# Chunked attention by pairs of tiles, with its 64x64 products on all four quarters of the array

## The chip, the cores and the metric

One core of one Trainium2 chip runs one program. The metric is the device time of that core in microseconds (us), as the median of several runs. TensorE is called PE below (PEld is its weight load), VectorE DVE, ScalarE ACT, GpSimd POOL, and SP is the engine that issues most of the DMAs.

## The reference

Three stages follow each other; only the first is touched by the change. Attention is taken within chunks of 64 positions, apart for each of 8 batches and 8 heads:

```python
q_c = q.reshape(B, H, nc, 64, D)            # B, H, S, D = 8, 8, 576, 64, float32; k_c, v_c alike
scores = scale * np.matmul(q_c, k_c.transpose(0, 1, 2, 4, 3))
attn = np.exp(scores - np.max(scores, axis=-1, keepdims=True))
attn = attn / (np.sum(attn, axis=-1, keepdims=True) + 1e-09)
out = np.matmul(attn, v_c)                  # then heads side by side: x of [8, 576, 512]
```

The second stage, called the mixing here, shifts `x` by one position, blends it with two vectors, and multiplies by `w_k` (512x1024), `w_v` (1024x512) and `w_r` (512x512): `sigmoid(xr @ w_r) * (relu(xk @ w_k)**2 @ w_v)`. The third stage gates 4 experts, each a causal attention over all 576 positions with a head of 64.

## The kernel before

A **tile** is 128 positions, so two chunks `c` of 64, with all 8 heads, which are kept as 4 pairs `g` of two heads `e`. There are 36 tiles. For a tile the kernel runs four steps:

- `s_T` transposes q and k on PE (4 + 4 products with the identity) into PSUM and copies them to SBUF on ACT. Each transposed tile has head `e` of a pair on partitions 64e to 64e+63. k is copied in two halves into a buffer `KB` that holds zeros outside two diagonal blocks, so that one product with 128 rows gives the scores of both heads of a pair.
- `s_S` makes the scores: 8 products (4 pairs of heads, 2 chunks) of 128 rows, 64 columns of weights and 128 columns that stream; chunk `c` lands on partitions 64c to 64c+63. DVE then takes the maximum (L158), subtracts it (L160), ACT takes the exponential (L161), DVE sums (L163), adds 1e-9 (L164), inverts (L165), and DVE or POOL multiplies (L166).
- `s_PT` transposes the result (4 products) and ACT copies it.
- `s_PV` multiplies with v: 16 products of 64 rows, 64 columns of weights and 64 streamed columns. In each, rows and output partitions belong to the same head `e`, so only the two quarters of the array on its diagonal are used. ACT copies the result into the unit's `XT`.

All of these are float32. The trace shows two records on PE for each float32 product that is not a transpose, and one for a transpose: 16 for the scores of a tile, 32 for its products with v.

A **unit** is 384 positions, three tiles; there are 12. The mixing of a unit is 240 products of 128 rows, 128 columns of weights and 384 streamed columns, in lines L57 to L59 (tile `mps`); 2,880 in all. Its weights come from HBM as 64-bit floats and are made into two 32-bit parts by 40 **conversions** of 128x256, four DVE instructions each (L290, L291, L292, L294), besides work on ACT and POOL. Conversions, attention and the mixing of unit 0 are interleaved at the start of the program. After that a credit per mixing item (`rate0`, `rate`; 20 items a unit) lets attention steps in, up to `xb` = 4 units ahead. The list `attn` holds the steps with a lag of two tiles: T of tile t, PT of t-2, S of t, PV of t-2. A scheduler that works with a timeline of its own moves instructions within this; on the chip each engine runs its instructions in the order that it wrote.

PSUM has eight banks: three for the mixing, and five for attention, given as 3 for transposes, 1 for scores, 1 for products with v.

Of the kernel before, what the change touches and what calls it, by code (L numbers as in the profile page):

```python
# [8 lines left out]
F32 = mybir.dt.float32  # L9
F32R = mybir.dt.float32r  # L10
# [10 lines left out]
CH = 64  # L21
UNIT = 384
CFG = dict(ps=(2, 3, 1, 2), P=5, sm=3, load=6, lag=(3, 4), out=(5, 1), qk1=(1, 1), qk0=(10, 1.2), v=(11, 1), order=(3, 4, 0, 1, 2), after=1, conv='v', clo='g', x2hi='g', x2lo='v', ylo='g', yhi='v', xt='aa', r2='av', klo='vg', slo='gv', d='gg', amul='vg', nearly=2, x2b=1, yb=4, qb=4, direct=((0, 1), (1, 1), (1, 1)), tailAV=4, kp=1, yt=1, yf=2, zb=1, om=(4, 3, 2, 1, 0), hp=1000, x2d=2, early=3, rate0=0.65, rate=0.7, sh=(10, 12, 2), sh2=(11, 1, -1), pro=(24, 0.4, 20, 18), alag=2, seq=0, end=2, outL=(10, 2), outE=2, first='qqcvcvcv', kcp='aa', dsc='v', ldb=2, vb=3, cn=256, stb=3, xb=4, pa=(3, 1, 1), cb=2)
# [38 lines left out]
def attn_mix(tc, at, x2T, q, k, v, mu_k, mu_r, w_k, w_v, w_r, ident, attended_all, mixed_k):  # L62
# [14 lines left out]
    with ExitStack() as ctx:  # L77
# [28 lines left out]
        def load_v(t):  # L106
            x = at.tile([128, 2, HP, D], F32, tag="ldv", bufs=CFG["vb"], name="ldv")
            for c in range(2):
                b, s = divmod(t * 128 + c * CH, S)
                for e in range(2):  # L110
                    nc.sync.dma_start(out=x[e * 64:(e + 1) * 64, c],
                                      in_=v[b, e::2, s:s + CH, :].rearrange("g p d -> p g d"))
            qkv["v", t] = x

        qT, kT, PP, PT, XT = {}, {}, {}, {}, {}

        KB = [at.tile([128, HP, 2, 128], F32, tag=f"kT{i}", bufs=1, name="kT") for i in range(2)]
        for x in KB:
            for e in range(2):
                r = slice(e * 64, e * 64 + 64)  # L120
                nc.gpsimd.memset(x[r, :, :, 64 - e * 64:128 - e * 64], 0.0)
        seen = []
        nT = NU * TPU

        def s_T(t):
            with tc.issue_after(seen[-1].ins) if seen and t < CFG["seq"] else nullcontext():
                s_T2(t)

        def s_T2(t):
            for nm, dst in (("q", qT), ("k", kT)):  # L130
                src = qkv.pop((nm, t))
                p = pa.tile([128, HP, 128], F32, tag="T", bufs=CFG["pa"][0], name="Tps")
                for g in range(HP):
                    nc.tensor.transpose(p[:, g], src[:, g * 128:(g + 1) * 128], ident)  # L134
                if nm == "q":
                    o = at.tile([128, HP, 128], F32, tag="qT", name="qT")
                    nc.scalar.activation(out=o, in_=p, func=ACTF.Copy)
                else:
                    o = KB[t % 2]
                    for e in range(2):  # L140
                        r = slice(e * 64, e * 64 + 64)
                        copy(nc, CFG["kcp"][e], o[r, :, :, r], p[r].rearrange("p g (c k) -> p g c k", c=2))
                dst[t] = o
            if t + CFG["ldb"] < nT:
                load_qk(t + CFG["ldb"])

        def s_S(t):
            a, b = qT.pop(t), kT.pop(t)
            p = pa.tile([128, H * CH], F32, tag="S", bufs=CFG["pa"][1], name="Sps")
            for g in range(HP):  # L150
# [4 lines left out]
            p = p.rearrange("p (h k) -> p h k", h=H)  # L155
            seen.append(last)
            m = at.tile([128, H], F32, tag="m", name="m")
            nc.vector.tensor_reduce(m, p, axis=AXX, op=ALU.max)  # L158
            e = at.tile([128, H, CH], F32, tag="P", name="P")
            nc.vector.tensor_tensor(e, p, m.unsqueeze(2).to_broadcast([128, H, CH]), op=ALU.subtract)  # L160
            nc.scalar.activation(out=e, in_=e, func=ACTF.Exp, scale=scale)  # L161
            z = at.tile([128, H], F32, tag="z", name="z")
            nc.vector.tensor_reduce(z, e, axis=AXX, op=ALU.add)  # L163
            nc.vector.tensor_scalar(z, z, 1e-9, None, op0=ALU.add)  # L164
            nc.vector.reciprocal(z, z)  # L165
            eng(nc, CFG["amul"][t // TPU >= CFG["nearly"]]).tensor_tensor(e, e, z.unsqueeze(2).to_broadcast([128, H, CH]), op=ALU.mult)  # L166
            PP[t] = e

        def s_PT(t):
            e = PP.pop(t).rearrange("p h k -> p (h k)")  # L170
            p = pa.tile([128, HP, 128], F32, tag="T", bufs=CFG["pa"][0], name="PTps")
            for g in range(HP):
                nc.tensor.transpose(p[:, g], e[:, g * 128:(g + 1) * 128], ident)
            o = at.tile([128, HP, 128], F32, tag="PT", name="PT")
            nc.scalar.activation(out=o, in_=p, func=ACTF.Copy)
            PT[t] = o

        def s_PV(t):
            a = PT.pop(t)
            vt = qkv.pop(("v", t))  # L180
            p = pa.tile([128, HP, 128], F32, tag="PV", bufs=CFG["pa"][2], name="PVps")
            for g in range(HP):
                for c in range(2):
                    for e in range(2):
                        r = slice(e * 64, e * 64 + 64)
                        cc = slice(c * CH, (c + 1) * CH)
                        nc.tensor.matmul(out=p[r, g, cc], lhsT=vt[r, c, g], rhs=a[r, g, cc],  # L187
                                         start=True, stop=True)
            u, i = divmod(t, TPU)
            if i == 0:  # L190
                XT[u] = wkr.tile([128, HP, NSEG, SEG + 1], F32, tag="XT", bufs=CFG["xb"], name="XT")
            x = XT[u]
            g0, done = i * 2, 0
            while done < 2:
                sg, o = divmod(g0 + done, CPS)
                n = min(2 - done, CPS - o)
                copy(nc, CFG["xt"][u >= CFG["nearly"]], x[:, :, sg, 1 + o * CH:1 + (o + n) * CH], p[:, :, done * CH:(done + n) * CH])
                done += n
            if t + CFG["vb"] < nT:
                load_v(t + CFG["vb"])  # L200
# [119 lines left out]
        lag = CFG["alag"]  # L320
        for t in range(nT + lag):
            if t < nT:
                attn.append((t // TPU, s_T, t))
            if t >= lag:
                attn.append(((t - lag) // TPU, s_PT, t - lag))
            if t < nT:
                attn.append((t // TPU, s_S, t))
            if t >= lag:
# [550 lines left out]
```

## Time and profile before

| | us |
|---|---|
| median of 3 runs (1089.34 to 1090.14) | 1089.36 |
| the profiled execution, its own time | 1086.98 |
| span of its trace | 1085.2 |
| TensorE busy | 1040.5 |
| VectorE busy | 747.2 |
| ScalarE busy | 612.9 |
| GpSimd busy | 451.4 |

The span is the time from the first to the last instruction in the trace. Busy time is the union of an engine's instructions; TensorE's instructions are pipelined, so the start of one to the start of the next says what one costs, and not its own duration.

### The profile page before, as it was taken

How to read it: one execution, taken by the hardware profiler on the slowest of the kernel's cores; microseconds unless marked ns; L12 is line 12 of the kernel's file. 1: busy time of each engine (PE TensorE's matmuls, PEld its weight loads, DVE VectorE, ACT ScalarE, POOL GpSimd, SP SyncE). 2: the span in 40 equal slices, each digit the busy share in tenths (PEclk: the TensorE clock that was granted, in tenths of full speed). 3: DMA queues.
4: the chain of work that ended last, by engine and by line, in shares of the span. 5: the costliest groups of instructions: out<-in, count | busy, mean ns of one | idle time of the engine just before them, and what ended most of it. 6: DMA issues, size and time to landing. Idle time of an engine off the chain costs nothing.

```text
span 1085.2 us, 21428 instructions
## 1 busy us (share of the span) xinstructions
PE 1040.5 (96%) x7846; PEld 979.8 (90%) x7846; DVE 747.2 (69%) x1910; ACT 612.9 (56%) x1457; POOL 451.4 (42%) x569
## 2 busy tenths in 40 slices
PE   5788899999999999999999999999999999999997
PEld 4676689999999999999999999999999898999985
DVE  5999994465554746463646652488697787878996
ACT  5778767242244646363535324266776667666774
POOL 2574663355553535353535453632331232423101
PEclk8999999999999999999999999999999999999999
DMA  9847673101103232414121311852742535254312
GB/s 194 202 105 177 178 187 89 59 1 59 53 17 93 55 98 50 111 41 112 40 69 24 85 44 35 178 149 54 182 119 85 150 66 178 56 160 114 89 52 70
DMA packets 170401, 105.23 MB, mean 97 GB/s; under 512 B 133832, under 2 KB 146232, under 8 KB 170296
## 3 DMA queue, kind: packets, MB, share of 16 engines
q1 hardware_dynamic: 134904, 54.56, 20.2%
q0 software_dynamic: 35392, 49.30, 17.3%
q8 instruction: 63, 1.03, 0.4%
q14 instruction: 42, 0.34, 0.1%
HBM read 66.01 MB, written 28.38 MB: 87 GB/s over the span
## 4 chain that ended last, share of the span: by engine, by line
PE 70%; DVE 16%; DMA 5%; ACT 3%; issue 3%; SPq 2%; POOL 1%; ACTq 0%; DVEq 0%; POOLq 0%
PE mps L57 14%; PE mps L59 14%; PE mps L58 14%; PE pj L57 4%; PE pj L58 4%; PE pj L59 4%; PE Tps L654 3%; PE PVps L187 2%; PE AVps L678 2%; PE Sps L153 2%; DMA out_dram<-o 2%; PE AVps L674 2%; PE Tps L134 2%; DVE sm L596 1%; PE Sps L594 1%
## 5 line engine op out<-in xcount | busy, mean ns | idle before, releaser
L218 POOL TENSOR_TENSOR xa<-XT 128x384 f32<-128x384 f32 x96 | 92.7, 974 | 106.2 <-DVE xlr L229 75.6
L57 PE MATMUL mps<-xhk,wkh 128*128 128x384 f32 x384 | 132.1, 345 | 1.8 <-ACT wkh L306 1.8
L57 PE MATMUL mps<-kh,wvh 128*128 128x384 f32 x384 | 130.1, 345 | 1.4 <-ACT wvh L306 1.4
L58 PE MATMUL mps<-xlk,wkh 128*128 128x384 f32 x384 | 129.6, 337 | 0.0
L59 PE MATMUL mps<-xhk,wkl 128*128 128x384 f32 x384 | 128.9, 340 | 0.0
L59 PE MATMUL mps<-kh,wvl 128*128 128x384 f32 x384 | 127.5, 338 | 0.7 <-POOL wvl L307 0.7
L58 PE MATMUL mps<-kl,wvh 128*128 128x384 f32 x384 | 127.7, 336 | 0.0
L256 DVE TENSOR_TENSOR r<-r 128x384 f32<-128x384 f32 x80 | 68.0, 850 | 68.2 <-ACT r L249 68.0
L258 POOL TENSOR_TENSOR kl<-r,kh 128x384 fp32r<-128x384 f32 x80 | 86.7, 1086 | 65.4 <-ACT kh L257 60.9
L606 ACT ACTIVATE P<-sm,nm 128x128 f32<-128x128 f32 (+4 forms) x160 | 91.3, 571 | 37.9 <-DVE nm L596 22.2
L227 DVE SCALAR_TENSOR_TENSOR xa<-xa,mu,XT 128x384 f32<-128x384 f32 x96 | 88.8, 939 | 19.5 <-POOL xa L218 19.4
L596 DVE CUSTOM_DVE_ANT_0 sm<-Sps,mask 128x192 f32<-128x192 f32 (+3 forms) x192 | 83.5, 438 | 14.0 <-PE Sps L594 12.2
L257 ACT ACTIVATE kh<-r 128x384 fp32r<-128x384 f32 x96 | 50.5, 526 | 63.8 <-DVE r L256 63.4
L654 PE MATMUL Tps<-ident,P 128*128 128x128 f32 x480 | 81.3, 275 | 1.7 <-DVE PT00l L658 0.8
L515 POOL DMA_DIRECT2D K<-Kp x64 | 34.2, 547 | 110.7 <-ACT Kp L508 110.1
L57 PEld LDWEIGHTS mps<-xhk,wkh 128*128 128x128 f32 x384 | 72.1, 188 | 4.2 <-ACT wkh L306 2.5
L57 PEld LDWEIGHTS mps<-kh,wvh 128*128 128x128 f32 x384 | 71.9, 188 | 4.2 <-ACT wvh L306 2.0
L59 PEld LDWEIGHTS mps<-kh,wvl 128*128 128x128 f32 x384 | 71.5, 188 | 1.6 <-POOL wvl L307 0.9
L59 PEld LDWEIGHTS mps<-xhk,wkl 128*128 128x128 f32 x384 | 72.1, 189 | 0.9 <-issue 0.3
L58 PEld LDWEIGHTS mps<-xlk,wkh 128*128 128x128 f32 x384 | 72.3, 188 | 0.3 <-issue 0.2
L58 PEld LDWEIGHTS mps<-kl,wvh 128*128 128x128 f32 x384 | 72.1, 188 | 0.2 <-issue 0.2
L57 PE MATMUL mps<-xhr,wrh 128*128 128x384 f32 x192 | 66.3, 351 | 3.0 <-ACT sig L242 2.1
(198 smaller groups left out, 3038.0 us busy)
## 6 DMA issues: line engine op xcount, KB each, us to landing
x2T<-x2d POOLq DMA_DIRECT2D x48, 384.0 KB, 2.8
x<-x2T POOLq DMA_DIRECT2D x32, 576.0 KB, 6.2
ldv<-in_v_dram SPq DMA_DIRECT2D x144, 64.0 KB
K<-Kp POOLq DMA_DIRECT2D x64, 144.0 KB, 3.0
ldq<-in_q_dram SPq DMA_DIRECT2D x32, 256.0 KB
ldk<-in_k_dram SPq DMA_DIRECT2D x32, 256.0 KB
out_dram<-o SPq DMA_DIRECT2D x32, 256.0 KB
st<-in_moe_w_k_dram SPq DMA_DIRECT2D x16, 256.0 KB
```

The costliest lines, as they stand in the source:

```text
L57: nc.tensor.matmul(out=out, lhsT=ah, rhs=bh, start=first and i == 0, stop=False)
L58: nc.tensor.matmul(out=out, lhsT=ah, rhs=bl, start=False, stop=False)
L59: nc.tensor.matmul(out=out, lhsT=al, rhs=bh, start=False, stop=last and i == n - 1)
L218: eng(nc, CFG["d"][late]).tensor_tensor(d, now, prev, op=ALU.subtract)
L227: nc.vector.scalar_tensor_tensor(a, d, mu[:, w, g:g + 1], prev, op0=ALU.mult, op1=ALU.add)
L256: eng(nc, CFG["r2"][u >= CFG["nearly"]]).tensor_tensor(r2, r, r, op=ALU.mult)
L257: nc.scalar.activation(out=o.hi, in_=r2, func=ACTF.Copy)
L258: eng(nc, CFG["klo"][u >= CFG["nearly"]]).tensor_tensor(o.lo, r2, f32(o.hi), op=ALU.subtract)
L515: nc.gpsimd.dma_start(out=d[half[j]], in_=t[half[i]])
L596: nc.vector.tensor_tensor_reduce(out=sm[:n, a:a + w], in0=pp[:n, :w], in1=mk[:, a:a + w], op0=ALU.add, op1=ALU.min, scale=-scale, scalar=3e38,
L606: nc.scalar.activation(out=x[:n, :nk], in_=sm[:n, :nk], func=ACTF.Exp, scale=-1.0, bias=nm[:n, :1], accum_out=z)
L654: nc.tensor.transpose(pp[:, j - j0], x[:, o:o + 128], ident)
```

## The change

Attention goes by pairs of tiles. `s_S(j)` makes the scores of tiles 2j and 2j+1 with 32 products for each pair of heads and chunks taken apart: 64 rows, 64 columns of weights, 64 streamed columns. The four products of a pair of heads (two heads `e`, two chunks `c`) have four different pairs of row half and column half, and the products that stand on one diagonal go to one PSUM bank, those on the other diagonal to another. `s_PV(j)` does the same: v is loaded so that chunk 1 has its heads on exchanged partitions. The new step `s_SPV(j)` puts the scores of pair j directly ahead of the products with v of pair j-1. The zero-padded `KB` is gone, and k is copied by one ACT instruction, as q. The five PSUM banks of attention become one ring of five. DVE's maximum and subtraction stay one per bank, two for a pair; sum, addition, inverse and product are one for a pair. The credits are reset for the smaller number of steps (`rate0` 0.65 to 0.43, `rate` 0.7 to 0.45), and so is the start (`pro`: 24 rounds of attention with 0.4 conversions each become 17 with 0.56; the first shift comes after round 14 and not 18).

```diff
-            for g in range(HP):
-                for c in range(2):
-                    cc = slice(c * CH, (c + 1) * CH)
-                    last = nc.tensor.matmul(out=p[cc, g * 128:(g + 1) * 128], lhsT=a[:, g, cc], rhs=b[:, g, c],
-                                            start=True, stop=True)
...
+        def s_S(j):
+            banks = [bank("Sps").rearrange("p g (i k) -> p i g k", i=2) for _ in range(2)]
+            for i in range(2):
+                a, b = qT.pop(2 * j + i), kT.pop(2 * j + i)
+                for g in range(HP):
+                    for c in range(2):
+                        for o in range(2):
+                            e = o ^ c
+                            r, cc = slice(e * 64, e * 64 + 64), slice(c * CH, (c + 1) * CH)
+                            with tc.high_priority(1000) if j < CFG["first_j"] else nullcontext():
+                                nc.tensor.matmul(out=banks[o][cc, i, g], lhsT=a[r, g, cc], rhs=b[r, g, cc],
+                                                 start=True, stop=True)
...
+            for o, p in enumerate(banks):
+                nc.vector.tensor_reduce(m[:, o], p, axis=AXX, op=ALU.max)
+                nc.vector.tensor_tensor(e[:, :, :, o], p, m[:, o].unsqueeze(3).to_broadcast([128, 2, HP, CH]),
+                                        op=ALU.subtract)
...
+                            e = o ^ c
+                            r, cc = slice(o * 64, o * 64 + 64), slice(c * CH, (c + 1) * CH)
+                            with tc.high_priority(1000) if j < CFG["first_j"] else nullcontext():
+                                nc.tensor.matmul(out=banks[c][e * 64:e * 64 + 64, i, g], lhsT=vt[r, c, g],
+                                                 rhs=a[r, g, cc], start=True, stop=True)
...
+        for j in range(nT // 2 + 1):
+            two = (2 * j, 2 * j + 1)
+            attn += [(t // TPU, s_T, t) for t in two if t < nT]
+            attn += [((t - 2) // TPU, s_PT, t - 2) for t in two if t > 1]
+            attn.append(((2 * j - 1) // TPU if j else 0, s_SPV, j))
```

What the scheduler makes of it is seen in the order of the instructions. The first place is PE's queue near the start of the program, before: transposes (`Tps`, `PTps`), scores (`Sps`) and products with v (`PVps`) of one tile after the other.

```order
L153 MATMUL Sps<-kT,qT 64x128 x8
L187 MATMUL PVps<-PT,ldv 64x64 x16
L134 MATMUL Tps<-ident,ldk 128x128 x4
L173 MATMUL PTps<-ident,P 128x128 x4
L134 MATMUL Tps<-ident,ldq 128x128 x4
L153 MATMUL Sps<-kT,qT 64x128 x8
```

The same place with the change:

```order
L126 MATMUL Tps<-ident,P 128x128 x5
L153 MATMUL Sps<-kT,qT 64x64 x32
L183 MATMUL PVps<-PT,ldv 64x64 x16
L126 MATMUL Tps<-ident,P 128x128 x3
L126 MATMUL Tps<-ident,ldq 128x128 x4
```

The 64-row products now stand in longer runs: over the program 86 runs of such products, bounded by transposes or by the mixing, become 25.

The second place is PE's queue in the mixing of unit 5 before, where the scores and, 24 products later, the products with v of a tile stand alone among the products of the mixing (`mps`):

```order
L58 MATMUL mps<-xlk,wkh 128x384
L59 MATMUL mps<-xhk,wkl 128x384
L153 MATMUL Sps<-kT,qT 64x128 x8
L57 MATMUL mps<-xhk,wkh 128x384
L58 MATMUL mps<-xlk,wkh 128x384
```

```order
L58 MATMUL mps<-xlk,wkh 128x384
L59 MATMUL mps<-xhk,wkl 128x384
L187 MATMUL PVps<-PT,ldv 64x64 x16
L57 MATMUL mps<-xhk,wkh 128x384
L58 MATMUL mps<-xlk,wkh 128x384
```

With the change, in the same unit, a pair's scores and the products with v of the pair before stand in one run, and the next transposes come 36 to 48 products of the mixing behind it:

```order
L153 MATMUL Sps<-kT,qT 64x64 x32
L183 MATMUL PVps<-PT,ldv 64x64 x32
L57 MATMUL mps<-kh,wvh 128x384
L58 MATMUL mps<-kl,wvh 128x384
L59 MATMUL mps<-kh,wvl 128x384
```

The third place is DVE's queue at the last conversion of the program (the last row with `cz`), before:

```order
L290 TENSOR_SCALAR cb<-st 128x256
L291 SCALAR_TENSOR_TENSOR cb<-st,cb 128x256
L294 SCALAR_TENSOR_TENSOR cz<-cz,cb 128x256
L292 SCALAR_TENSOR_TENSOR cb<-st,cb 128x256
L158 TENSOR_REDUCE m<-Sps 128x8
L294 SCALAR_TENSOR_TENSOR cz<-cz,cb 128x256
L160 TENSOR_TENSOR P<-Sps,m 128x512
```

And with the change:

```order
L158 TENSOR_REDUCE m<-Sps 128x8 x2
L302 SCALAR_TENSOR_TENSOR cz<-cz,cb 128x256
L159 TENSOR_TENSOR P<-Sps,m 128x8x64 x2
L164 TENSOR_REDUCE z<-P 128x16
L165 TENSOR_SCALAR z<-z 128x16
L166 RECIPROCAL z<-z 128x16
```

Ahead of the last conversion DVE has, before, 20 maxima, 19 subtractions, 19 sums and 19 each of the two small steps; with the change 14 maxima, 12 subtractions, 6 sums (each of a pair) and 6 each of the two small steps. DVE's six multiplications by the inverse (L166) become three of twice the size. What is moved behind the last conversion is done later, among the mixing of later units. From product 252 of the mixing on, PE has 128 products for scores, 289 with v and 192 transposes in the order of before, in 38 runs of 64-row products and 33 of transposes; with the change 352, 400 and 264, in 13 runs and 48. From a little behind the end of attention on, the order is the same on all engines.

## Rows read from the trace of the kernel before

**Rows 1.** Busy time, share of the span and instructions of each engine.

```profile
PE 1040.5 (96%) x7846; PEld 979.8 (90%) x7846; DVE 747.2 (69%) x1910; ACT 612.9 (56%) x1457; POOL 451.4 (42%) x569
```

**Rows 2.** Busy time in stretches: from:to, length, each engine, clock, DMA share, GB/s.

```profile
0.00:24.00 24.00, 13.29 (x83) 10.20 (x84) 11.40 (x28) 11.71 (x22) 7.19 (x17) 0.79 0.91 194
24.00:167.30 143.30, 123.76 (x1306) 103.06 (x1306) 139.74 (x270) 105.76 (x231) 86.28 (x99) 0.96 0.70 170
167.30:588.00 420.70, 420.70 (x3070) 406.05 (x3070) 231.77 (x354) 196.94 (x374) 194.64 (x225) 1.00 0.23 60
700.00:1085.20 385.20, 371.79 (x2741) 350.13 (x2739) 310.36 (x1172) 261.74 (x750) 105.54 (x151) 1.00 0.40 109
```

**Rows 3.** Timeline of DVE around the last conversion: start, us, instruction, [idle before].

```profile
163.32 0.43 DVE L294 SCALAR_TENSOR_TENSOR cz<-cz,cb 128x256 f32<-128x256 f32 x1 [0.36 <-ACT cz L289]
...
165.37 0.69 DVE L163 TENSOR_REDUCE z<-P 128x8 f32<-128x512 f32 x1 [1.02 <-ACT P L161]
```

**Rows 4.** DVE's attention instructions from 24 to 167.3: count, busy us, mean ns.

```profile
L160 DVE TENSOR_TENSOR P<-Sps,m 128x512 f32<-128x512 f32 x18 | 12.2, 680 | 0.0
L163 DVE TENSOR_REDUCE z<-P 128x8 f32<-128x512 f32 x18 | 12.2, 676 | 1.0 <-ACT P L161 1.0
L158 DVE TENSOR_REDUCE m<-Sps 128x8 f32<-128x512 f32 x18 | 12.1, 673 | 0.3 <-PE Sps L153 0.3
...
L164 DVE TENSOR_SCALAR z<-z 128x8 f32<-128x8 f32 x18 | 5.2, 288 | 0.0
...
L165 DVE RECIPROCAL z<-z 128x8 f32<-128x8 f32 x18 | 3.5, 194 | 0.1
```

**Rows 5.** Timeline of DVE: two neighbours and the distance of their starts.

```profile
28.97 0.68 DVE L158 TENSOR_REDUCE m<-Sps 128x8 f32<-128x512 f32 x1
29.57 0.70 DVE L164 TENSOR_SCALAR z<-z 128x8 f32<-128x8 f32 x1
```

**Rows 6.** The mixing's products from 167.3 to 588.

```profile
167.30:588.00 420.70, 373.06 (x2044) 352.28 (x2044) 18.47 (x34) 51.28 (x106) 1.00 0.23 60
```

**Rows 7.** Timeline of PE: the pace of the mixing.

```profile
212.40 0.34 PE L58 MATMUL mps<-xlr,wrh 128*128 128x384 f32 x1
...
214.14 0.34 PE L59 MATMUL mps<-xhr,wrl 128*128 128x384 f32 x1
```

**Rows 8.** Timeline of PE: one product with v, alone between products of the mixing.

```profile
214.41 0.33 PE L187 MATMUL PVps<-PT,ldv 64*64 64x64 f32 x2
...
214.94 0.34 PE L58 MATMUL mps<-xlr,wrh 128*128 128x384 f32 x1
```

**Rows 9.** Timeline of PE: a run of 16 products with v.

```profile
399.92 0.34 PE L59 MATMUL mps<-xhr,wrl 128*128 128x384 f32 x1
400.19 1.15 PE L187 MATMUL PVps<-PT,ldv 64*64 64x64 f32 x32
...
401.54 0.34 PE L58 MATMUL mps<-xlr,wrh 128*128 128x384 f32 x1
```

**Rows 10.** Timeline of PE: a run of 8 products for scores.

```profile
396.61 0.34 PE L59 MATMUL mps<-xhr,wrl 128*128 128x384 f32 x1
396.88 1.09 PE L153 MATMUL Sps<-kT,qT 128*64 128x128 f32 x16
...
398.18 0.34 PE L58 MATMUL mps<-xlr,wrh 128*128 128x384 f32 x1
```

**Rows 11.** Timeline of PE: a run of 4 transposes.

```profile
391.96 0.34 PE L59 MATMUL mps<-kh,wvl 128*128 128x384 f32 x1
392.14 0.60 PE L173 MATMUL PTps<-ident,P 128*128 128x128 f32 x4
...
392.76 0.34 PE L58 MATMUL mps<-kl,wvh 128*128 128x384 f32 x1
```

**Rows 12.** One record of a product with v: count, busy us, mean ns.

```profile
L187 PE MATMUL PVps<-PT,ldv 64*64 64x64 f32 x578 | 21.6, 221 | 0.0
```

**Rows 13.** DMA from 0 to 167.3.

```profile
DMA packets 76865, 29.03 MB, mean 174 GB/s; under 512 B 71214, under 2 KB 71726, under 8 KB 76846
```

More of the change, by code (lines that the diff above doesn't have):

```diff
@@ L129, in s_T2 @@
[L129 to L132, printed above, removed]
-                for g in range(HP):
[L134 to L143, printed above, removed]
+        nT = NU * TPU
@@ new lines, in bank, with to_sbuf @@
+        def bank(nm):
+            return pa.tile([128, HP, 128], F32, tag="A", bufs=CFG["pa"], name=nm)
+        def to_sbuf(src, nm):
+            p = bank("Tps")
+            for g in range(HP):
+                nc.tensor.transpose(p[:, g], src[:, g * 128:(g + 1) * 128], ident)
+            o = at.tile([128, HP, 128], F32, tag=nm, bufs=CFG["tb"], name=nm)
+            nc.scalar.activation(out=o, in_=p, func=ACTF.Copy)
+            return o
+        def s_T(t):
+            qT[t] = to_sbuf(qkv.pop(("q", t)), "qT")
+            kT[t] = to_sbuf(qkv.pop(("k", t)), "kT")
@@ L144, in s_T2, with s_PT @@
             if t + CFG["ldb"] < nT:
                 load_qk(t + CFG["ldb"])
[L147 to L150, printed above, removed]
-                for c in range(2):
-                    cc = slice(c * CH, (c + 1) * CH)
-                    last = nc.tensor.matmul(out=p[cc, g * 128:(g + 1) * 128], lhsT=a[:, g, cc], rhs=b[:, g, c],
-                                            start=True, stop=True)
[L155 to L163, printed above, removed]
+        def s_PT(t):
+            PT[t] = to_sbuf(PP.pop(t).rearrange("p g o k -> p (g o k)"), "PT")
@@ L178, in s_PV @@
[L178 to L200, printed above, removed]
+            eng(nc, CFG["amul"][2 * j // TPU >= CFG["nearly"]]).tensor_tensor(
+                ef, ef, z.unsqueeze(2).to_broadcast([128, 2 * H, CH]), op=ALU.mult)
@@ new lines, in s_S, with s_PV @@
+            for i in range(2):
+                PP[2 * j + i] = e[:, i]
+        def s_PV(j):
+            banks = [bank("PVps").rearrange("p g (i k) -> p i g k", i=2) for _ in range(2)]
+            for i in range(2):
+                t = 2 * j + i
+                a, vt = PT.pop(t), qkv.pop(("v", t))
+                for g in range(HP):
+                    for c in range(2):
+                        for o in range(2):
+                            e = o ^ c
[3 more added lines that the diff above has]
+                                                 rhs=a[r, g, cc], start=True, stop=True)
+            for c, p in enumerate(banks):
+                done = 0
+                while done < 2:
+                    (u, k), n = divmod(4 * j + c + 2 * done, CH_U), 1
+                    if u not in XT:
+                        XT[u] = wkr.tile([128, HP, NSEG, SEG + 1], F32, tag="XT", bufs=CFG["xb"], name="XT")
+                    sg, o = divmod(k, CPS)
+                    if done == 0 and o + 2 < CPS:
+                        n = 2
+                    dst = XT[u][:, :, sg, 1:].rearrange("p g (w q) -> p w g q", q=CH)[:, o:o + 2 * n - 1:2]
+                    copy(nc, CFG["xt"][u >= CFG["nearly"]], dst, p[:, done:done + n])
+                    done += n
+            for i in range(2):
+                if 2 * j + i + CFG["vb"] < nT:
+                    load_v(2 * j + i + CFG["vb"])
```

53 lines of the change are left out of this document (19 added, 34 removed).

## Prediction

> **What bounds the kernel now.** First the busy times of the whole: PE is busy for 96% of the span, but VectorE has 69% too [rows 1], so the stages have to be taken apart. The table by stretches does that [rows 2]. In the first stretch, to 24 us, the loads rule (DMA share 0.91). From 24 to 167.3 us DVE is busy for 139.7 of 143.3 us while PE has gaps; I chose 167.3 as the end because there product 252 of the mixing starts, and the last conversion of a weight stands just ahead, at 163.3 us [rows 3]. From 167.3 to 588, where attention ends, PE is busy for all of 420.7 us and DVE for 231.8. Behind that the program is unchanged. So there are two parts that the change can move: a first one that ends when DVE has done 40 conversions and whatever attention stands ahead of the last of them, and a second one that ends when PE has done its queue. The change moves work from one to the other, and that must be counted on both sides.
>
> **First part: DVE.** Ahead of the last conversion the changed order has 6 maxima, 7 subtractions and 7 tiles' worth of sums fewer, and 13 fewer of each of the two small steps (19 of a tile against 6 of a pair). With the means of [rows 4] that is 6 x 0.673 + 7 x 0.680 + 7 x 0.676 + 13 x (0.288 + 0.194) = 4.0 + 4.8 + 4.7 + 6.3 = 19.8 us. Neighbours on DVE overlap by some 0.08 us: two starts are 0.60 apart where the first lasts 0.68 [rows 5]. For 33 instructions that takes back 2.6, so 17.2 us. Against it, the sum of a pair now stands directly behind the subtraction in places, with the exponential of both tiles between them; before, such a wait was 1.02 us once [rows 3]. Six pairs, some of them with conversions to fill the gap: between 0 and 6 us, and I take 3. The three larger multiplications cost what the six did. The first part should shrink by 14 us; bounds 9 (the waits in full, and two more at the start, where the first attention work needs a pair's loads) and 19.
>
> Could something else hold the first part? DMA has a share of 0.70 in it [rows 2] and moved 29.0 MB by its end [rows 13]. Six tiles of q, k and v are loaded later, at 3 x 128 x 512 x 4 bytes each, 4.7 MB; 24.3 MB in 153 us is 159 GB/s against 174 now, so it is not pressed harder. ACT is busy for 105.8 of 143.3 us and loses one of two k copies per tile. PE loses work. Each has room, so ACT's saving is priced at nothing: what hides it is DVE here and PE later.
>
> **Second part: PE.** Prices are read from starts. The mixing's pace is 0.174 us: ten steps from 212.40 to 214.14 [rows 7]. One product with v alone makes 214.14 to 214.94, 0.80 us, out of two such steps: it costs 0.80 - 0.348 = 0.452 [rows 7, 8]. Its two records together last 0.33, one lasts 0.22 [rows 8, 12], so the second starts 0.11 behind the first. Thus a lone product holds its quarter for 0.11, and 0.345 is the price of going into 64-row products and out. A run of 16 costs 401.54 - 399.92 - 0.348 = 1.272 [rows 9]; less 0.345 that is 0.058 for each: two products at a time, on the two diagonal quarters. A run of 8 for scores costs 1.222 [rows 10], so 0.110 each at 128 streamed columns. Four transposes cost 0.452 [rows 11], 0.109 each and 0.016 for the run.
>
> Check: the stretch holds 2,044 products of the mixing [rows 6], 355.7 us, and attention of 38 x 0.345 + 128 x 0.110 + 289 x 0.058 + 192 x 0.109 + 33 x 0.016 = 13.1 + 14.1 + 16.8 + 20.9 + 0.5 = 65.4. The sum is 421.1, and the stretch is 420.7.
>
> With the change the same part has 752 products of 64x64 in 13 runs and 264 transposes in 48 runs. What one costs when four quarters are filled in turn is not in the trace. Upper bound: 0.058, no gain over two quarters. Lower bound: 0.029, if the other diagonal runs beside the first as its two quarters do beside each other. I take 0.029, since the resources that it needs are already used this way: scores now stream two different right sides through the same rows into two column halves at once (0.110 per product, while one pass of 128 columns takes 0.109 in a transpose), and products with v use two row halves at once. Then 13 x 0.345 + 752 x 0.029 + 264 x 0.109 + 48 x 0.016 = 4.5 + 21.8 + 28.8 + 0.8 = 55.9 us, 9.5 less than 65.4, although six tiles more are done here. At 0.058 it is 77.7, so 12.3 more.
>
> The TensorE page of the Trainium skill ("TensorE: Matmul & The Clock Gate", in "Wait — 56ns, not 53.3ns?") says that matmuls never start less than about 25 ns apart, however few columns. By that a product of two records costs an estimated 0.050, and the sum is 71.7 us, 6.3 more than before. The trace agrees only so far as its densest stretch has 0.029 per record [rows 9]; pairs that start almost together are not ruled out by it.
>
> **Sum.** -14 - 9.5 = -23.5 us. The profiled execution took 1086.98, 1.8 over its span and 2.4 under the median of 1089.36; I put the difference on the median: 1066.
>
> **Rivals.**
> 1. Records come to the array more slowly than four quarters could take them. For: the change asks for twice the densest pace in the trace. Against: 0.029 per record is just what two quarters allow, so no limit of issue has been seen. Half way between the bounds, 0.044, the second part costs 67.2, 1.8 more than before, and the time is 1089.4 - 14 + 1.8 = 1077. By the page's figure it would be 1081.7.
> 2. The change does not do what it says: two products at a time, as before. For: the two halves of one output column half now come from two row halves at once, which no row shows. The merged runs still save 25 x 0.345 = 8.6, but the moved tiles are paid on PE: -14 + 12.3 = -1.7, so 1087.7, within 0.2%.
> 3. The side of slower: PE waits for a bank. The ring of five means that transposes of the next pair need the bank of this pair's scores, free only after two maxima and the subtractions, 4 x 0.68 = 2.7 us of DVE, which is in order and does other work between. Cover: 36 to 48 products of the mixing, 6.3 to 8.3 us. DVE is busy for 55% of the stretch [rows 2], so 2.7 us should be had in some 6. What is queued behind such a wait on PE is the mixing itself. It decides from a wait of (23.5 + 2.2) / 11 = 2.3 us at each of 11 pairs; at 3 us it costs 33 and the time is 1099.
> 4. The first part doesn't shrink, because its conversions wait for loads or pairs arrive late at the start. Then only -9.5: 1080.
>
> **Chances.** Forecast 0.52; rival 1 0.20; rival 2 0.13; rival 3 0.07; rival 4 0.08. About 0.2% (2.2 us) is what a measurement can tell from no change. Faster: the forecast, rivals 1 and 4, less a little for mixtures, 0.79. Same: most of rival 2, 0.10. Slower: rival 3 and some of rival 2, 0.11. The forecast's own range is 1061 to 1071 from the first part's bounds; with rivals 1 and 4 and half of rival 2 it reaches from 1058 to 1087.
>
> **What would show it.** Right: PE's run of a pair's 64 products, with the entry, takes some 0.345 + 64 x 0.029 = 2.2 us between products of the mixing (4.1 if only two go at a time, 3.2 at 0.044); the last conversion falls near 149 us and product 252 of the mixing near 153; PE stays fully busy from there to the end of attention, and that stretch is some 10 us shorter, near 411. Wrong: PE waiting for DVE's L159 or ACT's copies of `PVps` in that stretch; DVE idle in the first part ahead of the sum L164; or a run of 64-row products as dense as before.

## The result, and the profile after

The changed kernel takes 1074.14 us (median of 4, 1072.51 to 1074.93) against 1089.75 for the kernel before in the same comparison (median of 4, 1089.34 to 1092.59): a ratio of 0.985 [0.983, 0.987], so 15.6 us or 1.5% faster. The profiled execution took 1074.6 us with a span of 1072.8 us. The forecast was 1066 with a range of 1058 to 1087: the range holds the time, the forecast's own range of 1061 to 1071 does not.

The busy times of the whole, and the table by stretches (from:to, length, PE, weight loads, DVE, ACT, POOL, clock, DMA share, GB/s), cut where product 252 of the mixing starts, at 157.7 us:

```profile
PE 1004.7 (94%) x8422; PEld 959.2 (89%) x8422; DVE 749.8 (70%) x1853; ACT 586.0 (55%) x1413; POOL 448.0 (42%) x550
...
24.00:157.90 133.90, 98.09 (x1124) 86.90 (x1124) 127.58 (x221) 77.50 (x178) 77.67 (x85) 0.82 0.57 142
157.90:574.00 416.10, 412.62 (x3810) 404.29 (x3810) 246.71 (x354) 200.78 (x390) 202.03 (x224) 1.00 0.31 74
...
686.00:1072.80 386.80, 373.69 (x2758) 352.31 (x2758) 312.21 (x1175) 263.49 (x753) 105.89 (x151) 1.00 0.40 109
```

Beside [rows 2] the reader is to see three things. The first part is DVE's as before (127.6 of 133.9 us busy), and PE has more gaps in it: its granted clock fell from 0.96 to 0.82 there. DVE sets this part's end, and its longer waits there are for ACT (3.3 us) and for DMA (2.0 us), none for PE, so the lower clock should cost little; no run tests that. In the second part PE is no longer busy throughout: 3.5 us of it are idle, where before there was none. And the last row is that of before within 2 us.

Product 252 starts at 157.7 instead of 167.1 us (-9.4; forecast -14). The stretch from there to the end of product 2292 of the mixing is 416.3 instead of 420.3 us (-4.0; forecast -9.5). Behind it the program takes 498.8 instead of 497.8. The three add up to the 12.4 us between the two profiled spans. The medians are 15.6 apart, as the profiled execution of the kernel before was 2.8 us under its median and that of the changed kernel 0.5 over.

The timeline of PE around one pair's run (start, us, instruction, count of records; a product makes two):

```profile
261.17 0.34 PE L59 MATMUL mps<-xhk,wkl 128*128 128x384 f32 x1
261.44 1.16 PE L153 MATMUL Sps<-kT,qT 64*64 64x64 f32 x64
262.42 1.18 PE L183 MATMUL PVps<-PT,ldv 64*64 64x64 f32 x64
...
263.82 0.34 PE L58 MATMUL mps<-xlk,wkh 128*128 128x384 f32 x1
```

As in [rows 9], the cost is the distance of the products of the mixing around it less two of their steps: 263.82 - 261.17 - 0.348 = 2.30 us for 64 products and the entry. The eleven such runs give 2.23 to 2.30. The forecast was 2.2 on four quarters, 4.1 on two, 3.2 half way. So the array does what the change wants of it, and the price of a product is right. What was missed lies mostly beside it.

**First part.** The groups of DVE from 24 to 157.9 us (count, busy us, mean ns, idle before and what ended it): the four instructions of a conversion, and the subtraction, which reads PSUM:

```profile
L299 DVE SCALAR_TENSOR_TENSOR cb<-st,cb 128x256 int32<-128x256 int32 x37 | 27.0, 739 | 0.4
L302 DVE SCALAR_TENSOR_TENSOR cz<-cz,cb 128x256 f32<-128x256 f32 x37 | 24.0, 662 | 2.0 <-ACT cz L297 1.7
L300 DVE SCALAR_TENSOR_TENSOR cb<-st,cb 128x256 int32<-128x256 int32 x37 | 22.4, 613 | 0.2
L298 DVE TENSOR_SCALAR cb<-st 128x256 int32<-128x256 int32 x37 | 16.2, 439 | 2.1 <-DMA st<-in_moe_w_k_dram 1.4 <-DMA st<-in_moe_w_r_dram 0.3 <-DMA st<-in_moe_w_v_dram 0.3
...
L159 DVE TENSOR_TENSOR P<-Sps,m 128x512 f32<-128x512 f32 x12 | 7.8, 680 | 0.0
```

The same four of the kernel before, from 24 to 167.3 us:

```profile
L292 DVE SCALAR_TENSOR_TENSOR cb<-st,cb 128x256 int32<-128x256 int32 x37 | 24.3, 658 | 0.3
L294 DVE SCALAR_TENSOR_TENSOR cz<-cz,cb 128x256 f32<-128x256 f32 x37 | 21.5, 582 | 0.4 <-ACT cz L289 0.4
L291 DVE SCALAR_TENSOR_TENSOR cb<-st,cb 128x256 int32<-128x256 int32 x36 | 21.1, 587 | 0.1
L290 DVE TENSOR_SCALAR cb<-st 128x256 int32<-128x256 int32 x36 | 17.9, 498 | 1.3 <-DMA st<-in_moe_w_r_dram 0.9 <-DMA st<-in_moe_w_k_dram 0.4
```

The conversions' code did not change, but one now costs 739 + 662 + 613 + 439 = 2453 ns against 2325. Over 37 of them that is 4.7 us, about what is missing. The subtraction has kept its 0.68 us [rows 4]. The rise stands in the instances that meet POOL. Of L299, L300 and L302 (before L291, L292 and L294) those that start outside a POOL instruction take 0.41 us on average in both traces, 58 before and 63 after; those that start inside one take 0.84 before (51) and 1.01 after (48). So they don't meet POOL more often, and POOL's share of the part is 0.58 against 0.60; each one that does is held for longer. What a conversion's instruction waits for is seen in the timeline of DVE

```profile
64.72 0.41 DVE L300 SCALAR_TENSOR_TENSOR cb<-st,cb 128x256 int32<-128x256 int32 x1
65.05 1.28 DVE L159 TENSOR_TENSOR P<-Sps,m 128x512 f32<-128x512 f32 x2
...
66.78 1.05 DVE L299 SCALAR_TENSOR_TENSOR cb<-st,cb 128x256 int32<-128x256 int32 x1
67.75 0.41 DVE L302 SCALAR_TENSOR_TENSOR cz<-cz,cb 128x256 f32<-128x256 f32 x1
68.08 1.21 DVE L300 SCALAR_TENSOR_TENSOR cb<-st,cb 128x256 int32<-128x256 int32 x1
```

beside that of POOL:

```profile
65.23 1.01 POOL L237 TENSOR_TENSOR xlk<-xa,xhk 128x384 fp32r<-128x384 f32 x1 [1.05 <-ACT xhk L236]
66.32 1.22 POOL L226 TENSOR_TENSOR xa<-XT 128x384 f32<-128x384 f32 x1
67.91 1.10 POOL L237 TENSOR_TENSOR xlk<-xa,xhk 128x384 fp32r<-128x384 f32 x1 [0.37 <-ACT xhk L236]
```

With POOL idle, L300 takes 0.41 us (at 64.72). The L299 that starts at 66.78, inside POOL's L226, ends at 67.83, 0.29 behind POOL's end at 67.54; the L300 at 68.08 ends at 69.29, 0.28 behind POOL's end at 69.01. Of the 48 that start inside a POOL instruction, 38 are held in this way, to 0.8 us or more. The L302 that starts at 67.75, just ahead of POOL's, is not held. Nor is the PSUM reader L159: two in 1.28 us with POOL at work over most of it. The Trainium skill ("SBUF — State Buffer", section "SBUF: two separate sides") says that VectorE and GpSimd share a pair of SBUF ports as an exclusive lock: an instruction of VectorE with two SBUF inputs (if that of GpSimd reads SBUF), or in a two-port mode, and one of GpSimd don't share the bandwidth, and the later one is blocked for the whole of the other. The trace agrees for these two instances, with 0.29 and 0.28 us of own time left behind POOL's end.

The timeline of DVE around the last conversion, beside [rows 3]:

```profile
154.06 0.41 DVE L302 SCALAR_TENSOR_TENSOR cz<-cz,cb 128x256 f32<-128x256 f32 x1
...
157.26 1.22 DVE L164 TENSOR_REDUCE z<-P 128x16 f32<-128x1024 f32 x1 [1.59 <-ACT P L162]
```

It falls at 154.1 where 149 was forecast. The sum of a pair waits for the exponential of both tiles, as said, but only this once in the first part; all of DVE's gaps there are 6.3 us against 3.6 before, so the 3 us allowed for waits was fair.

**Second part.** What PE waited for from 157.9 to 574 us, where the stretch ends (us in total, times, longest):

```profile
PE mps L58 <- POOL kl L266: 2.1, 3, 0.9
PE mps L57 <- DVE x2o L281: 1.0, 1, 1.0
PE mps L57 <- ACT kh L265: 0.2, 1, 0.2
```

And from there to 690 us:

```profile
PE mps L57 <- DVE x2o L281: 2.3, 3, 0.8
```

None of these is attention's own ring: L281 frees a PSUM bank of the mixing, and L265 and L266 make the operands of its third product. The three waits behind the stretch come after attention has ended on PE. Ahead of two of them, L281 stands in DVE's queue behind work on the third stage's weights, which waits for ACT and through it for a load:

```profile
595.82 0.42 DVE L436 TENSOR_TENSOR wv<-wst,wv 128x256 fp32r<-128x256 f32 x1 [2.43 <-ACT wv L435]
596.16 0.55 DVE L281 TENSOR_TENSOR x2o<-mps,sig 128x384 f32<-128x384 f32 x1
```

The timeline of DVE ahead of the one wait for L281 inside the stretch

```profile
397.10 0.56 DVE L284 TENSOR_TENSOR x2d<-x2o,x2d 128x384 fp32r<-128x384 f32 x1 [3.05 <-POOL x2d L46]
397.57 1.28 DVE L159 TENSOR_TENSOR P<-Sps,m 128x512 f32<-128x512 f32 x2
399.98 1.22 DVE L164 TENSOR_REDUCE z<-P 128x16 f32<-128x1024 f32 x1 [1.13 <-ACT P L162]
...
403.55 0.55 DVE L281 TENSOR_TENSOR x2o<-mps,sig 128x384 f32<-128x384 f32 x1
```

and the row of PE behind it:

```profile
404.15 0.44 PE L57 MATMUL mps<-xhr,wrh 128*128 128x384 f32 x1 [1.05 <-DVE x2o L281]
```

From the subtractions' start to the end of L281, DVE's queue runs for 6.5 us, 1.1 of it idle while ACT makes the exponential of two tiles (L162); the mixing's bank is freed behind all that, and PE stands for 1.05 us. But DVE has stood once before, 3.05 us ahead of L284, for a copy of POOL's that waits for a transfer. In the second profile of the same kernel (e13_after) the same instructions come in the same order, with the first stop shorter and the second as long:

```profile
393.86 0.56 DVE L284 TENSOR_TENSOR x2d<-x2o,x2d 128x384 fp32r<-128x384 f32 x1 [1.19 <-POOL x2d L46]
...
396.75 1.22 DVE L164 TENSOR_REDUCE z<-P 128x16 f32<-128x1024 f32 x1 [1.13 <-ACT P L162]
```

There PE does not wait for L281. So the stop at the exponential alone does not make this wait; it adds to another. The three waits for kl begin 14 to 18 us behind the start of a pair's sum, among DVE's and POOL's work on the mixing's operands; what share the pair has in them, no run tells apart.

Two groups of DVE's, from 157.9 to 574 us:

```profile
L164 DVE TENSOR_REDUCE z<-P 128x16 f32<-128x1024 f32 x12 | 14.6, 1220 | 15.7 <-ACT P L162 15.7
L264 DVE TENSOR_TENSOR r<-r 128x384 f32<-128x384 f32 x61 | 54.5, 893 | 57.2 <-ACT r L257 57.2
```

A pair's sum stands for 1.3 us each of 12 times in an engine that works in order. L264, the square that kh and kl are made from, stands in the same queue. DVE is busy for 59% of this stretch, against 55% before, and before PE did not wait in it.

### The profile page after: what moved, and what is told of

It is laid out like the page before. It is cut to its first block, busy times and chain, and to the rows that moved or that the text cites. A ratio compares the mean times of both kernels' runs of the same rounds, so it can differ in the third digit from the quotient of the medians.

```text
span 1072.8 us, 22466 instructions
## 1 busy us (share of the span) xinstructions
PE 1004.7 (94%) x8422; PEld 959.2 (89%) x8422; DVE 749.8 (70%) x1853; ACT 586.0 (55%) x1413; POOL 448.0 (42%) x550
## 4 chain that ended last, share of the span: by engine, by line
PE 64%; DVE 21%; DMA 5%; ACT 4%; issue 4%; SPq 2%; POOL 1%; ACTq 0%; DVEq 0%; POOLq 0%
PE mps L57 12%; PE mps L59 12%; PE mps L58 12%; PE pj L57 5%; PE pj L58 4%; PE pj L59 4%; PE Tps L656 3%; PE AVps L680 2%; PE Tps L126 2%; DVE cb L299 2%; DVE xa L235 2%; PE AVps L676 2%; PE Sps L596 2%; PE Sps L595 2%; DVE cz L302 2%
## 5 line engine op out<-in xcount | busy, mean ns | idle before, releaser
L226 POOL TENSOR_TENSOR xa<-XT 128x384 f32<-128x384 f32 x96 | 95.1, 999 | 88.8 <-DVE xlr L237 46.8
L264 DVE TENSOR_TENSOR r<-r 128x384 f32<-128x384 f32 x80 | 68.6, 858 | 83.1 <-ACT r L257 83.0
L266 POOL TENSOR_TENSOR kl<-r,kh 128x384 fp32r<-128x384 f32 x80 | 87.8, 1102 | 82.1 <-ACT kh L265 81.1
L235 DVE SCALAR_TENSOR_TENSOR xa<-xa,mu,XT 128x384 f32<-128x384 f32 x96 | 85.8, 907 | 15.1 <-POOL xa L226 15.1
L265 ACT ACTIVATE kh<-r 128x384 fp32r<-128x384 f32 x96 | 50.3, 524 | 62.2 <-DVE r L264 61.8
```

Of the source, the lines that this page charges most:

```text
L226: eng(nc, CFG["d"][late]).tensor_tensor(d, now, prev, op=ALU.subtract)
L235: nc.vector.scalar_tensor_tensor(a, d, mu[:, w, g:g + 1], prev, op0=ALU.mult, op1=ALU.add)
L264: eng(nc, CFG["r2"][u >= CFG["nearly"]]).tensor_tensor(r2, r, r, op=ALU.mult)
L265: nc.scalar.activation(out=o.hi, in_=r2, func=ACTF.Copy)
L266: eng(nc, CFG["klo"][u >= CFG["nearly"]]).tensor_tensor(o.lo, r2, f32(o.hi), op=ALU.subtract)
```

## The experiments

Each kernel is the changed one with the edit shown, but for the one made from the kernel before. Ratios are against the kernel before, run on the same chip. The three columns behind it are the start of product 252, the stretch to product 2292 and PE's idle time in it, from the profile.

| kernel | median us | ratio | product 252 | stretch | PE idle |
|---|---|---|---|---|---|
| before (first profile) | 1089.75 | 1 | 167.1 | 420.3 | 0.0 |
| changed (first profile) | 1074.14 | 0.985 [0.983, 0.987] | 157.7 | 416.3 | 3.5 |
| e1_two | 1086.12 | 0.998 [0.997, 1.000] | 152.5 | 432.9 | 3.9 |
| e2_apart | 1075.93 | 0.989 [0.986, 0.991] | 159.9 | 414.7 | 1.2 |
| e4_r2a | 1068.68 | 0.982 [0.979, 0.985] | 156.4 | 412.6 | 0.7 |
| e6_clov | 1074.66 | 0.987 [0.985, 0.990] | 153.7 | 419.7 | 5.5 |
| e7_both | 1069.31 | 0.983 [0.981, 0.985] | 153.7 | 416.6 | 3.1 |
| e8_exp2 | 1072.74 | 0.986 [0.983, 0.988] | 155.8 | 413.2 | 4.7 |
| e9_before_r2a | 1088.22 | 0.999 [0.998, 1.001] | 167.0 | 420.6 | 0.0 |
| e10_fj5 | 1073.39 | 0.987 [0.984, 0.989] | 150.1 | 421.4 | 5.0 |
| e11_exp2_r2a | 1067.99 | 0.981 [0.980, 0.983] | 156.4 | 412.3 | 2.9 |
| e12_fj5_r2a | 1070.19 | 0.983 [0.982, 0.985] | 151.0 | 418.7 | 3.2 |
| e13_after | 1074.37 | 0.987 [0.986, 0.989] | 156.5 | 414.7 | 2.4 |

**e1_two: the same products, one diagonal after the other.**

```diff
-                for g in range(HP):
-                    for c in range(2):
-                        for o in range(2):
+            for o in range(2):
+                for i, (a, b) in enumerate(ab):
+                    for g in range(HP):
+                        for c in range(2):
...
-                for g in range(HP):
-                    for c in range(2):
+            for c in range(2):
+                for i, (a, vt) in enumerate(av):
+                    for g in range(HP):
```

> The same products in another order: all of one diagonal of the array first, then all of the other, so that neighbours in the queue use two quarters and not four. Theory (four quarters run at once, 0.029 us a product; two give 0.058): a run of 64 products takes 4.0 to 4.1 us and not 2.24, the stretch of the mixing is some 22 us longer, less a few that waits take back, and the time is 1091 to 1096. Rival (a product's cost does not hang on which quarters its neighbours use; the gain is that of longer runs): a run stays at 2.2 us and the time at 1074.

PE's timeline around a pair:

```profile
258.89 0.34 PE L59 MATMUL mps<-xhk,wkl 128*128 128x384 f32 x1
259.16 1.73 PE L153 MATMUL Sps<-kT,qT 64*64 64x64 f32 x58
260.68 0.27 PE L182 MATMUL PVps<-PT,ldv 64*64 64x64 f32 x2
260.73 0.28 PE L153 MATMUL Sps<-kT,qT 64*64 64x64 f32 x3
...
260.86 1.74 PE L182 MATMUL PVps<-PT,ldv 64*64 64x64 f32 x59
...
262.80 0.34 PE L58 MATMUL mps<-xlk,wkh 128*128 128x384 f32 x1
```

262.80 - 258.89 - 0.348 = 3.56 us against 2.30 with the same instructions in the other order. So four quarters do work at once, and rival 2 falls. It is less than the 4.0 to 4.1 expected: where one diagonal ends and the next begins, records of both are mixed (as at 260.68 and 260.73), so the two overlap a little. The stretch is 16.6 us longer. Product 252 came 5.2 us earlier than in the first profile of the changed kernel (4.0 earlier than in e13_after). Up to the last conversion, DVE spends 3.3 us less in the conversions' instructions than in the first profile, is idle for 3.5 us less and has two maxima fewer (1.4 us); what made these differ was not tested. That and the shorter runs are why the whole stayed under the 1091 to 1096 expected. The gain in time of the change is all but gone.

**e2_apart: scores and products with v as two runs.** The step of a pair is split in two, with the transposes of P between them, and the credits fit the larger number of steps.

```diff
+            if 2 * j < nT:
+                attn.append(((2 * j - 1) // TPU if j else 0, s_S, j))
             attn += [((t - 2) // TPU, s_PT, t - 2) for t in two if t > 1]
-            attn.append(((2 * j - 1) // TPU if j else 0, s_SPV, j))
+            if j:
+                attn.append(((2 * j - 1) // TPU, s_PV, j - 1))
```

> Scores and products with v as steps of their own, with the transposes between: 27 runs of 64x64 products behind product 252 of the mixing and not 13, two tiles more ahead of it. Theory (0.345 us for each entry into 64-row products): 14 x 0.345 = 4.8 us more on PE there, less some 4 for the two tiles that are moved ahead and cost as much on VectorE, so 1077 to 1080 with the second part's own count near 411 + 1. Rival (the entry is hidden by the loads of weights and only the number of products counts): 1074 or less, and a run of 32 scores costs under 1.0 us.

PE's timeline around a run of 32 products:

```profile
247.53 0.34 PE L59 MATMUL mps<-xhr,wrl 128*128 128x384 f32 x1
247.80 1.16 PE L153 MATMUL Sps<-kT,qT 64*64 64x64 f32 x64
...
249.17 0.34 PE L58 MATMUL mps<-xlr,wrh 128*128 128x384 f32 x1
```

1.64 - 0.348 = 1.292 us, so two runs cost 2.58 where one of 64 costs 2.23 to 2.30: the difference, 0.28 to 0.35, is close to the entry of 0.345, and 0.03 is left for a product. Both prices stand. 1075.93 is a little under what was expected. By the ratios it is 2 to 4 us behind the changed kernel (0.989 against 0.987 in e13_after and 0.985 in the first comparison), with intervals that overlap. The stretch shows nothing of a loss: PE idles less in it (1.2 us). What the profile is longer by lies ahead of product 252 (2.2 us) and behind the stretch (3.0 us); that execution was the longest of the four.

**e4_r2a: the mixing's square on ACT.**

```diff
-r2='av'
+r2='aa'
```

> The square of the mixing in later units on ScalarE and not VectorE (0.89 us each, 61 of them from 157.9 to 574). Theory (the 5 us of PE waits in that stretch are of VectorE's queue, which is blocked while it waits for a pair's exponential): VectorE has 54 us less to do there, the wait for L281 falls from 3.4 us to under 1, and the time to 1069 to 1072. Rival (the waits come from the chain relu, square, split, which is as long on ScalarE, whose queue holds the pair's exponential and copies too): the waits stay or move to L266, 1073 to 1078.

The second stretch, and what PE waited for from 158 to 590 us:

```profile
157.90:574.00 416.10, 415.39 (x3803) 408.52 (x3801) 209.34 (x292) 235.05 (x460) 194.57 (x226) 1.00 0.31 74
PE mps L58 <- POOL kl L266: 0.6, 1, 0.6
PE mps L57 <- DVE x2o L281: 0.6, 1, 0.6
```

DVE loses 37 us of work there (54 had been expected) and ACT gains 34. PE's idle time in the stretch falls from 3.5 us (2.4 in e13_after) to 0.7, and the waits for kl from 2.1 and 2.0 to 0.6; the one for L281 in the rows above lies behind the stretch, at 584 us. The stretch is 412.6. So PE's waits in it hang on the work in DVE's queue and in the chain from r to kl. The missing wait for L281 says nothing by itself, as it is missing from e13_after too.

**e9_before_r2a: the same edit in the kernel before.** The diff is that of e4_r2a.

> The kernel before, with the square of later units on ScalarE. Theory (PE never waits in the second part of the kernel before, so VectorE's load there costs nothing; the waits came with the pairs): no change, ratio 0.998 to 1.002. Rival (the edit gains by itself, whatever the attention): a ratio of 0.996 or less.

No change, and PE busy throughout the stretch as before. So the square on DVE cost nothing until attention went by pairs: the waits came with the change.

**e6_clov: the lower halves of the weights by DVE, not POOL.**

```diff
-clo='g'
+clo='v'
```

> The low part of each converted weight is taken on VectorE and not on GpSimd: 40 instructions more on VectorE, 40 of 0.84 us fewer on GpSimd, the rest in the same order. Theory (a conversion's instruction takes 0.42 us when GpSimd is idle and 1.0 when it works, so the first part pays some 0.48 us for each us of GpSimd work): +12 us of work, -15 us of slowing, so the last conversion comes 0 to 6 us earlier and the mean of L299 falls from 0.74 to near 0.55. Rival (GpSimd does not matter; VectorE is only a sum of its instructions): the last conversion comes 10 to 13 us later, 1084 to 1087.

DVE's groups from 24 to 153.9 us:

```profile
L302 DVE SCALAR_TENSOR_TENSOR cz<-cz,cb 128x256 f32<-128x256 f32 x37 | 22.0, 598 | 0.4 <-ACT cz L297 0.2
L300 DVE SCALAR_TENSOR_TENSOR cb<-st,cb 128x256 int32<-128x256 int32 x37 | 20.1, 548 | 0.1
L299 DVE SCALAR_TENSOR_TENSOR cb<-st,cb 128x256 int32<-128x256 int32 x37 | 16.3, 446 | 0.1
L298 DVE TENSOR_SCALAR cb<-st 128x256 int32<-128x256 int32 x37 | 13.6, 369 | 1.3 <-DMA st<-in_moe_w_k_dram 1.1
```

A conversion's four take 1961 ns instead of 2453, and the last one ends 4.4 us earlier than in the first profile (2.6 than in e13_after), although DVE does about 40 instructions more. POOL is busy for 48.4 us there instead of 77.7, and 25 instances of L299, L300 and L302 start inside one of its instructions instead of 48; the 86 that don't take 0.41 us as ever. So it is POOL's work that makes them slow. The gain is given back behind it: PE idles 2.0 us longer in the stretch, and 11 transposes fewer lie ahead of product 252 (1.2 us at 0.109); the whole stays where it was.

**e7_both: the edits of e4_r2a and e6_clov.**

> The low parts of converted weights on VectorE and the square of later units on ScalarE, together. Theory (the first edit ends the first part some 4 us earlier, and its loss behind that was VectorE's queue before L281, which the second edit empties): the gains add, first part 153 to 155, PE waits behind it under 1.5 us, 1064 to 1068 against 1087.6 for the kernel before, a ratio of 0.978 to 0.982. Rival (what is gained ahead is paid behind, since PE's queue is what counts in the end): the ratio stays at 0.982 to 0.985.

1069.31 us: the two don't add, and the ratio stays over the 0.978 to 0.982 expected. The stretch that had 412.6 with e4_r2a alone has 416.6, with 3.1 us of idle time.

**e8_exp2: exponential and sum for each bank.**

```diff
-            nc.scalar.activation(out=ef, in_=ef, func=ACTF.Exp, scale=scale)
...
-            nc.vector.tensor_reduce(z, ef, axis=AXX, op=ALU.add)
+            zo = z.rearrange("p (i g o) -> p i g o", i=2, o=2)
+            for o in range(2):
+                nc.scalar.activation(out=e[:, :, :, o], in_=e[:, :, :, o], func=ACTF.Exp, scale=scale)
+            for o in range(2):
+                nc.vector.tensor_reduce(zo[:, :, :, o], e[:, :, :, o], axis=AXX, op=ALU.add)
```

> A pair's exponential and sum in two halves, one for each bank, so that ScalarE starts behind the first subtraction; the scheduler then also puts some three tiles' products with v more ahead of product 252. Theory (VectorE stands still some 1.3 us per pair before L164 for the exponential of both tiles, and the product of the mixing's result, L281, is queued behind it): that idle time falls from 15.7 us to under 6, PE's wait for L281 from 3.4 us to under 1.5, and the time to 1068 to 1073. Rival (it is the amount of work on VectorE that makes L281 late, not the stop): waits stay at 3 us or more, 1073 to 1076.

DVE's group of sums from 155.8 to 574 us:

```profile
L167 DVE TENSOR_REDUCE z<-P 128x8 f32<-128x512 f32 x22 | 14.5, 684 | 7.1 <-ACT P L165 6.1
```

DVE's wait for the exponential falls from 15.7 to 6.1 us, but PE's waits in the stretch don't fall with it: 0.9 us for L281 (here L284) against 1.0, others for ACT and POOL come up, and PE idles 4.7 us against 3.5. So the expected tie between this stop and PE's waits is not shown, and the rival, that it is the amount of work on DVE, stands. The stretch is 3.1 us shorter, yet 16 transposes and 61 products of 64x64 more now stand ahead of it (1.7 + 1.8 us), which is as much. The ratios, 0.986 here and 0.985 and 0.987 for the changed kernel, have intervals that overlap: a gain is not shown.

**e10_fj5 and e12_fj5_r2a: two tiles fewer at the start.** The first without, the second with the edit of e4_r2a.

```diff
-first_j=7
+first_j=5
```

> The changed kernel with a raised priority for 5 pairs and not 7, so that two tiles fewer stand ahead of product 252. Theory (a tile costs some 2.2 us of VectorE ahead of the last conversion, and 2.3 to 2.4 us of PE behind it, now that four quarters work): first part 4 to 5 us shorter, second 4 to 5 longer, the time unchanged, 1072 to 1076. Rival (the first part is not bound by VectorE's sum): it stays at 157 to 158 and the time rises by 4 to 5 us.

> Raised priority for 5 pairs and the square of later units on ScalarE. Theory (moving two tiles behind product 252 is neutral in itself, but it adds VectorE work where PE waits for VectorE; with the square gone that wait goes): second part 417 to 418 and not 421.4, first part at 150 to 152, ratio 0.979 to 0.983. Rival (the second part pays for the tiles on PE in full and the first part's gain was chance): 0.984 to 0.987.

In e10_fj5 product 252 comes 7.6 us earlier (4 to 5 had been expected), the stretch grows by 5.1 and the rest by 1.5: a tile moved out of the first part shortens DVE's sum there and is paid for behind it. That the first part is DVE's sum is borne out; moving two tiles more won nothing. In both runs, as in e6_clov and e7_both, a wait for L281 of 1.4 to 2.1 us stands near product 252, 1.7 us behind the start of a pair's sum that has itself waited 1.1 to 1.6 us for its exponential: there the stop at the exponential is close ahead of the wait. With the square on ACT the stretch is 418.7 (417 to 418 had been expected) and the time 1070.19, not under e4_r2a.

**e11_exp2_r2a and e13_after: the edits of e8_exp2 and e4_r2a together, and the changed kernel once more.**

> The exponential and sum of a pair in halves, and the square of later units on ScalarE. Theory (both take from the same PE waits in the second part, of which 0.7 us were left with the second edit alone; the halves also let more attention stand ahead of product 252): at best 1 us under the square alone, ratio 0.980 to 0.983. Rival (the two edits take from different waits and add): 0.977 to 0.980.

> The changed kernel once more, beside the two others. All theories: a ratio of 0.983 to 0.987 to the kernel before, a first part of 157 to 158 us and PE waits of 3 to 5 us behind it, if these are the program's and not one execution's. Rival (they vary from one execution to the next): a first part off by 3 us or more, or waits under 1.5 us.

1067.99 (1066.63 to 1069.18) against 1074.37 (1072.31 to 1075.46) on the same chip: 6.4 us under the changed kernel and 0.981 of the kernel before, the best version with e4_r2a, from which it can't be told apart. In the stretch of e11_exp2_r2a PE idles 2.9 us, 1.9 of them in one wait for ACT's sigmoid. The second profile of the changed kernel has the last conversion 1.8 and product 252 1.2 us earlier; product 252 is at 156.5 where 157 to 158 had been expected. The three waits for kl are there again (2.0 us), so they are the program's; the one for L281 in the stretch is not. PE idles 2.4 us, where 3 to 5 had been expected. Behind the stretch there are three waits for L281 as in the first profile (1.8 us against 2.3). So one profile gives the size of these waits to within 1 us or so.

## Why the forecast came out as it did

The stated range holds the time because it left room for rivals that fell. Rival 1's 1077 is nearer to 1074 than the forecast's 1066, so the time alone would speak for rival 1; the price of a run speaks against it.

**The bound and the split into two parts** were right: DVE's sum ends the first part, PE's queue the second, and the work that moves between them is paid on both sides (e10_fj5).

**The price of a product on four quarters, 0.029 us, and that of an entry, 0.345**, were right to within 0.1 us a run: 2.23 to 2.30 us where 2.2 was forecast, and 3.56 as soon as the order leaves two quarters empty (e1_two). Rivals 1 and 2 fall. 128 records in 2.24 - 0.345 us are 0.015 each. The Trainium skill ("TensorE: Matmul & The Clock Gate", "Wait — 56ns, not 53.3ns?") has matmuls start no less than about 25 ns apart, by which rival 1 had a second price; for products on different quarters the trace does not agree, and the measurement decides.

**First part, -14: the step is right, its size is not (-9.4).** DVE's busy time there falls by 12.2 us (139.7 to 127.6) where 17.2 was summed, and its waits grow by 2.7 where 3 was allowed. Two things in the sum are behind the 5.0 us. It lacked that the conversions would not keep their mean durations: 4.7 us more. And it took the overlap of neighbours back for 33 instructions, while the terms that it lists are 6 + 7 + 13 + 13 + 13 = 52 fewer, so 4.2 us and not 2.6. With both mended it reads -19.8 + 4.2 + 4.7 + 2.7 = -8.2; the rest is about made up by the mixing's L235, which takes 0.78 us where L227 before took 0.87, 18 times. That POOL slows the conversions is shown (e6_clov, and the two groups of instances). Why each one that meets POOL is held for longer is argued: the maxima and subtractions taken out read PSUM and keep their 0.68 us, so they could run while POOL did, and the conversions now come up earlier within POOL's instructions. No run tests that.

**Second part, -9.5: measured -4.0 (-5.6 in e13_after).** The step that failed is that PE stays fully busy: it is idle for 3.5 us (2.4 in e13_after). I looked for a wait at attention's ring (rival 3) and priced nothing at the mixing's own operands and banks, although kl and L281 hang on DVE's queue, which attention shares. The other 2.0 us are not idle time of PE: the eleven runs of 64 products cost 0.05 us more each than summed, and the step behind a wait is longer than 0.174 (0.28 from 404.15 to the next product at 404.43); the rest is open. Even with the waits mostly gone (e4_r2a, 0.7 us idle) the stretch is 7.7 us shorter and not 9.5. Rival 3 was right that DVE, in order, is the place, wrong in the bank, and its waits are about a tenth of the 33 us that it had. e4_r2a takes most of them away and gains 3 to 6 us (0.982 against 0.985, where the intervals overlap, and against 0.987 in e13_after, where they don't); e9_before_r2a shows that they weren't there before. Which part of a pair's work on DVE makes them, the stop at the exponential or the amount in one piece, is not shown: e8_exp2 shortened the stop and not the waits, while in four runs a wait stands close behind such a stop (e10_fj5).

**Rival 4** had the first part not shrink at all, and fell.

Behind the stretch the program takes 1.0 us more where nothing was forecast; the waits there are 2.3 us against 0.6 before. Open are what in a pair's work makes the waits for kl, how the waits vary from one execution to the next (e13_after), why product 252 came so early in e1_two, and whether e8_exp2 gains anything by itself.

## What to carry to other kernels

A mean duration from the profile holds for the mix of work it was measured in: before it is carried over, see whether its instances fall in two groups, and what runs on the other engine in the slow one. When two small steps are merged, look at the engine that works in order and ask what is queued behind the larger step, above all work that frees another stage's buffers or makes its operands. And an order that only interleaves the same products over the array's quarters is worth a third of their time here (3.56 to 2.30 us), at no cost in instructions.

## What the runs showed of the hardware that was not expected

- A conversion's instruction with two inputs from SBUF takes 0.41 us on DVE when it starts outside a POOL instruction and 1.01 on average when it starts inside one (48 instances, 38 of them held, mostly to some 0.28 us behind POOL's end); the subtraction, which reads PSUM, stays at 0.68 either way.
- The records of 64x64 float32 products on four quarters go at 0.015 us each, with two records to a product.
- Going into 64-row products and out once more, where one run of 64 is split in two, costs 0.28 to 0.35 us (e2_apart). The Trainium skill ("TensorEngine Tiling (Array Packing)", section "Key Properties") says that a change of the array's mode drains it. The trace agrees in that the change costs time, and this is its size here.
